# A planned instruction order and in-place operands in a fused linear-attention and MLP kernel

## The chip, the core and the metric

The program runs on one core of a Trainium2 chip. The metric is the device time of one execution in microseconds (us), as the median of several runs. TensorE (PE) multiplies, VectorE (DVE) and ScalarE (ACT) do the elementwise work, GpSimd (POOL) a little of it, and SyncE (SP) only issues the transfers between HBM and the on-chip memory (SBUF).

## The reference

A block takes x (2048 tokens by 512), normalises each token, and adds to x the result of a 32-head linear attention and of a squared-ReLU MLP, both of the normalised tokens:

```python
xn = _layernorm(x, axis=-1)
return x + _A_ref(xn, A_wqkv, A_wo) + _B_ref(xn, B_w1, B_b1, B_w2, B_b2)
# A: q, k, v = xn @ wqkv;  phi(t) = where(t > 0, t + 1, exp(t)) + 1e-6
#    kv = phi(k)^T v per head;  z = sum over tokens of phi(k)
#    o = phi(q) kv / (phi(q) z + 1e-6);  result o @ wo
# B: h = xn @ w1 + b1;  relu(h)^2 @ w2 + b2     (1376 hidden units)
```

## The kernel before

**Arithmetic.** Everything is float32. Each matmul operand is split into a high part (an ACT copy to float32r) and a rest (a DVE subtraction); `split`, L108 and L116, does it everywhere. A product is then three passes of float32r matmuls of 128x128 by 128x512. The first projections of a pair of token blocks use Strassen's scheme with seven products instead of eight; for them the weights appear as seven operands per block of 256 columns (sums and differences of quarters, then split), called "1", k, i. The second projections use operands "2", k, i: four per block for the first pair of token blocks, more combinations for the second.

**Stages.** The 16 token tiles of 128 are normalised, turned and projected to k, and the sums `kx` over all tokens are made (L439). Then comes a loop over two pairs of token blocks, `n` = 0 and 1, 512 tokens to a block. In each pair, `p` runs over seven weight blocks: two of the q projection and five of w1. An iteration does seven products (L503), copies banks of PSUM out in steps (ACT L108, DVE L990, L998, L1026), applies phi or relu and square (L540, L543, L548, L549), splits the result (`s`), and multiplies it by the second operands (L521, `add_product`). For q the denominators are made by `shares` (L558 to L566). After the loop over p come the attention products, the remaining second products and the output: transposed on DVE (L870), added to the residual `res` (L872), and stored (L877).

**Operands.** All of the weights' operands are made once, by "pieces" (`prepare_1`, `prepare_2`, `prepare_z`, and `prepare_t` in the second pair): a load of raw rows into one of four slots (`raws`, L181, L198), sums on DVE (L242, L280, L281), the split into one of four staging slots (`st`), and a store to HBM (`spill`, L203, tensors `wd`, `wdz`). Both pairs then fetch each operand back from HBM (`fetch_ops`, L453) into a ring of eight one-operand slots, 256 KB each. So what the first pair uses makes the way to HBM and back too.

**Order.** Each engine runs its instructions strictly in the order in which the program lists them. That order is written out by hand: the loop calls `hook` at fixed places, and a table `PLAN` says for each place how many steps are taken from the queues "p" (pieces), "l" (denominators), "c" (combinations for the second pair) and "s" (token sums). In the token stage a table `PIECES` does the same. SP issues all transfers, in one queue. The PSUM has eight banks in two groups of four.

Of the kernel before, what the change touches and what calls it, by code (L numbers as in the profile page):

```python
# [14 lines left out]
H = 32  # L15


@with_exitstack
def kernel(
# [29 lines left out]
    nc = tc.nc  # L49
# [17 lines left out]
    nc.scalar.preload_act_table_set("natural_log_exp_and_others")  # L67

    keep = ctx.enter_context(tc.tile_pool(name="keep", bufs=1))
    work = ctx.enter_context(tc.tile_pool(name="work", bufs=1))  # L70
    small = ctx.enter_context(tc.tile_pool(name="small", bufs=4))
    psum = ctx.enter_context(tc.tile_pool(name="psum", bufs=4, space=bass.MemoryType.PSUM))
    ctx.enter_context(tc.manual_schedule())

    def bank(name, tag="ps"):
        return psum.tile([P, 512], F32, name=name, tag=tag)
# [4 lines left out]
    turns = {"x": [0, 2], "pair": [0, 5], "raw": [0, 4], "st": [0, 4]}  # L81
# [6 lines left out]
    def two(name):  # L88
        return keep.tile([P, 2, 512], F32, name=name, tag=next_tag("x"))
# [46 lines left out]
    xT = {b: keep.tile([P, NJ, BT], F32, name=f"xT{b}", tag=f"xT{b}") for b in range(NB // 2, NB)}  # L136
    first_xp = {i0: four(f"xp{i0}", tag, pool=keep) for i0, tag in zip(range(0, NT, TB), ("B0", "B1", "C0", "C1"))}
    for k in range(2):
        two(f"x_{k}")
    for k in range(5):  # L140
        pair(f"pair_{k}")
# [28 lines left out]
    raws = {}  # L170

    def turn_of(of):
        k, n = turns[of]
        turns[of][0] = (k + 1) % n
        return k

    def raw(name, src=None):
        k = turn_of("raw")
        t = raws[k // 2][:, k % 2]
        if src is not None:  # L180
            nc.sync.dma_start(t, src)  # L181
        return t

    stages = {}

    def stage():
        k = turn_of("st")
        return stages[k // 2][:, k % 2]
# [3 lines left out]

    def columns_of(w, f, n=P):
        t = raw("r")
        tj = t.rearrange("p (j n) -> p j n", j=NJ)
        if n < P:
            nc.gpsimd.memset(tj[:, :, n:], 0.0)
        nc.sync.dma_start(tj[:, :, :n], w[:, f * P:f * P + n].rearrange("(j p) n -> p j n", j=NJ))  # L198
        return t
# [6 lines left out]
    def ops_of(kind, k, i, src, el="dve"):  # L206

        n = src.shape[1]
        t = stage()[:, :n]
# [6 lines left out]
    def prepare_z(t, i, el="dve"):  # L216
        o = v = stage()
        if len(t.shape) == 4:
            v = o.rearrange("p u (h c m) -> p u h c m", h=2, c=2)
        split(v[:, 0], v[:, 1], t, "act", el)  # L220
        spill("z", 0, i, o)

    def prepare_z1():
        t = columns_of(w1, NF - 1, FL)
        return [lambda: prepare_z(t, 0)]

    def prepare_z2():
        t = raw("r")
        nc.gpsimd.memset(t[FL:, :], 0.0)
        nc.sync.dma_start(t[:FL, :], w2[(NF - 1) * P:, :])  # L230
        nc.sync.dma_start(t[FL:FL + 1, :], b2[None, :])
        return [lambda: prepare_z(by_chunks(by_halves(t)), 2)]

    def prepare_1(k, el="dve"):

        w, f = (wqkv, 2 * k) if k < NQ else (w1, 2 * (k - NQ))
        ra, rb = (columns_of(w, f + e).rearrange("p (h n) -> p h n", h=2) for e in range(2))
        a11, a12, a21, a22 = ra[:, 0], ra[:, 1], rb[:, 0], rb[:, 1]
        held_sums = {}

        def tt(o, x, y, op):
            nc.vector.tensor_tensor(out=o, in0=x, in1=y, op=op)  # L242

        def sums_12():
            o = held_sums[0] = sums_tile(f"sa{k}")
            tt(o[:, 0], a21, a22, OP.add)
            tt(o[:, 1], o[:, 0], a11, OP.subtract)
            ops_of("1", k, 2, o, el)

        def sums_34():  # L250
            o = sums_tile(f"sb{k}")
            tt(o[:, 0], a11, a21, OP.subtract)
            tt(o[:, 1], a12, held_sums[0][:, 1], OP.subtract)
            ops_of("1", k, 4, o, el)

        return [lambda: ops_of("1", k, 0, ra, el), sums_12, sums_34, lambda: ops_of("1", k, 6, rb[:, 1:], el)]
# [9 lines left out]
    def rows_of(k):  # L266
        at = [2 * k + e for e in range(2)] if k < NP else [2 * (k - NP) + e for e in range(2)]
        return [by_halves(raw("r", w2[f * P:(f + 1) * P, :] if k < NP else wdm[f])) for f in at]

    def prepare_2(k):  # L270
        t = rows_of(k)
        return [lambda e=e: ops_of("2", k, 2 * e, by_chunks(t[e])) for e in range(2)]

    def prepare_t(k):
        b1_, b2_ = rows_of(k)
        held_sums = {}

        def step(e, x, y, z, less):
            o = held_sums[e] = sums_tile(f"t{k}_{e}")
            nc.vector.tensor_tensor(out=o[:, 0], in0=x, in1=y, op=OP.subtract)  # L280
            nc.vector.tensor_tensor(out=o[:, 1], in0=z, in1=held_sums[0][:, less], op=OP.subtract)  # L281
            ops_of("2", k, 4 + 2 * e, by_chunks(o))

        return [lambda: step(0, b1_[:, 1], b1_[:, 0], b2_[:, 1], 0), lambda: step(1, b2_[:, 1], b1_[:, 1], b2_[:, 0], 1)]

    def piece_o(j):
        t = raw(f"ro{j}", wo[j * P:(j + 1) * P, :])
# [3 lines left out]
        return [lambda: split(*wos[j + 1], t, "act", "dve")]  # L291
# [151 lines left out]
    order, loaded, ready, op_slots, op_turn = [], [], set(), [], [0, 0]  # L443
# [4 lines left out]
    def fetch_ops():  # L448

        while order and op_turn[1] < len(op_slots) and order[0] in ready:  # L450
            key = order.pop(0)
            t = op_slots[op_turn[0] % 8]
            nc.sync.dma_start(f32(t), place_of(*key))  # L453
            loaded.append((key, t))
            op_turn[0] += 1
            op_turn[1] += 1

    def order_of(n):

        o = []  # L460
        for p in range(NK + 1):
            f = p - 1 - NQ
            if p < NK:
                o += [("1", p, i) for i in range(3)]
            if f >= 0:
                o += [("2", f, i) for i in ((0,) if n else (0, 1))]
            if p:
                o.append(("1", p - 1, 6))
            if p < NK:
                o += [("1", p, 3), ("1", p, 5)]  # L470
                if n and p == 0:
                    o += [("z", 0, u) for u in range(2)]
                if f >= 0:
                    o += [("2", f, i) for i in ((2,) if n else (2, 3))]
                o.append(("1", p, 4))
        attention = [("2", NP + j // 2, 2 * (j % 2) + v) for j in range(NJ) for v in range(2)]
        z = [("z", 0, 2 + u) for u in range(2)]

        def over(i):
            return [("2", f, i) for f in range(NP)]  # L480

        if n == 0:
            o += attention + [("2", NP - 1, i) for i in (2, 3)] + z
            return o + attention + [("2", f, i) for f in range(NP) for i in range(4)] + z
        o += over(4)[:-1] + [("2", NP - 1, 2), ("2", NP - 1, 4)]
        return o + attention + z + over(5) + over(3) + over(6) + attention + z + over(7)

    def op(*key):
        assert loaded, ("late", key)
        k, t = loaded.pop(0)  # L490
        assert k == key, (k, key)
        return t

    def used(n=1):
        op_turn[1] -= n
        fetch_ops()
# [19 lines left out]
    def second(ps, key, s, first=False, last=False):  # L516

        a = op(*key)
        for n, (u, v) in enumerate(ORDER):
            for c in range(2):  # L520
                nc.tensor.matmul(ps[c], lhsT=a[:, u * 256 + c * P:u * 256 + (c + 1) * P], rhs=s[:, v],  # L521
                                 start=first and n == 0, stop=last and n == 2, skip_group_check=True)
        used()

    def second_z(ps, cs, s, first=False, last=False):
# [6 lines left out]
        used(2)  # L532
# [197 lines left out]
    order.extend([("z", 0, u) for u in range(2)] + order_of(0) + order_of(1))  # L730
# [14 lines left out]
    def fetch():  # L745
        while todo and len(held) < 3:
            held.extend(todo.pop(0)())

    def pieces(n):
        for _ in range(n):  # L750
            if held:
                held.pop(0)()
            fetch()
# [450 lines left out]
```

## Time and profile before

| what | value |
|---|---|
| median of three runs | 514.56 us (513.11 to 516.28) |
| profiled execution, its own time | 518.54 us |
| its span, first to last instruction | 516.4 us |
| outside the span | 2.1 us |
| PE busy | 443.2 us, 86% of the span |
| DVE busy | 331.0 us, 64% |
| ACT busy | 255.6 us, 49% |
| moved by DMA | 117.45 MB, mean 227 GB/s |
| mean granted TensorE clock | 0.943 |

The profile gives for each engine its busy time, and for groups of instructions their number, mean duration and the idle time in front of them with what ended it ("<-"). `PEld` is the loading of weights, which overlaps PE. `x` counts instructions. A busy PE isn't necessarily at its peak, because matmuls overlap; the number of matmuls per stretch of time says more than the busy share.

### The profile page before, as it was taken

What the parts mean: (1) busy time and instruction counts of PE and PEld (TensorE: products, weight loads), DVE (VectorE), ACT (ScalarE), POOL (GpSimd) and SP (SyncE); (2) the same over time, 40 slices, a digit from 0 to 9 for tenths busy, and PEclk for the clock granted to TensorE, in tenths of its full rate; (3) what the DMA queues carried; (4) which work ended last, traced back from release to release, by engine and by line L of the source; (5) the groups of instructions that cost most, each with busy time, mean ns of one, the idle gap of its engine ahead of it and who ended that gap; (6) DMA issues with size and microseconds to landing.
All of it is one profiled execution on the core that took longest, in us unless ns stands there. A gap on an engine that the chain in (4) does not pass through costs nothing.

```text
span 516.4 us, 5845 instructions
## 1 busy us (share of the span) xinstructions
PE 443.2 (86%) x1808; PEld 346.0 (67%) x1808; DVE 331.0 (64%) x551; ACT 255.6 (49%) x438; POOL 28.1 (5%) x48
## 2 busy tenths in 40 slices
PE   8999799999778688897989998978867855899993
PEld 7787587877557566675858887855645633687781
DVE  6999869876555668675279405545855757336843
ACT  5765556564565644755156502554564466234310
POOL 2241223200000000000000000000000000000000
PEclk9999899999888897999879999989989898799998
DMA  7834556556899899999976877776447749956853
GB/s 251 272 104 124 187 170 193 163 181 203 280 382 348 327 384 392 330 387 285 210 216 187 237 225 193 215 248 217 150 137 268 218 152 231 197 182 191 216 164 81
DMA packets 96898, 117.45 MB, mean 227 GB/s; under 512 B 42242, under 2 KB 53506, under 8 KB 96612
## 3 DMA queue, kind: packets, MB, share of 16 engines
q1 hardware_dynamic: 96868, 117.09, 73.0%
q8 instruction: 14, 0.23, 0.2%
q14 instruction: 16, 0.13, 0.1%
HBM read 81.14 MB, written 33.82 MB: 223 GB/s over the span
## 4 chain that ended last, share of the span: by engine, by line
DVE 31%; PE 28%; ACT 16%; DMA 12%; issue 7%; SPq 4%; DVEq 0%; ACTq 0%
PE acc L521 13%; DMA raws<-in_B_w_dram 5%; DVE st L116 4%; DMA ops<-wd 4%; PE b L503 4%; PE Y L521 4%; ACT st L108 4%; ACT rr L540 2%; ACT s L108 2%; DVE s L116 2%; SPq L345 2%; PE V L521 2%; DVE o L870 2%; DVE st L301 1%; ACT rr L543 1%
## 5 line engine op out<-in xcount | busy, mean ns | idle before, releaser
L521 PE MATMUL acc<-s,ops 128*128 128x512 f32 x480 | 124.4, 414 | 6.5 <-ACT s L108 3.6
L521 PEld LDWEIGHTS acc<-s,ops 128*128 128x128 f32 x480 | 95.4, 201 | 32.9 <-ACT s L108 6.7
L503 PE MATMUL b<-T,ops 128*128 128x512 f32 x336 | 91.4, 414 | 19.4 <-DVE rr L990 14.3
L503 PEld LDWEIGHTS b<-T,ops 128*128 128x128 f32 x336 | 65.0, 198 | 40.9 <-DVE rr L990 17.6
L439 PE MATMUL kx<-pk,tok 128*128 128x512 f32 x192 | 48.1, 398 | 0.4 <-DVE pk L428 0.2
L116 DVE TENSOR_TENSOR s<-rr,s 128x512 fp32r<-128x512 f32 x46 | 29.7, 686 | 24.8 <-ACT s L108 24.8
L503 PE MATMUL b<-xs1h,ops 128*128 128x512 f32 x56 | 22.9, 450 | 24.4 <-ACT rr L108 14.9
L439 PEld LDWEIGHTS kx<-pk,tok 128*128 128x128 f32 x192 | 35.6, 190 | 9.6 <-DVE pk L428 1.2
L108 ACT ACTIVATE s<-rr 128x512 fp32r<-128x512 f32 x46 | 27.4, 628 | 28.6 <-PE acc L521 15.8
L503 PE MATMUL b<-xs0h,ops 128*128 128x512 f32 x112 | 37.0, 392 | 0.1
L503 PEld LDWEIGHTS b<-xs1h,ops 128*128 128x128 f32 x56 | 11.2, 200 | 31.2 <-ACT rr L108 18.0
L116 DVE TENSOR_TENSOR st<-raws,st 128x512 fp32r<-128x512 f32 (+1 forms) x30 | 21.9, 736 | 12.8 <-ACT st L108 10.9
L521 PE MATMUL Y<-s,ops 128*128 128x512 f32 x84 | 22.8, 422 | 6.7 <-ACT s L108 4.4
L116 POOL TENSOR_TENSOR tok<-xp,tok 128x512 fp32r<-128x512 f32 x16 | 23.4, 1467 | 60.6 <-ACT tok L108 56.5
L521 PEld LDWEIGHTS Y<-s,ops 128*128 128x128 f32 x84 | 16.8, 204 | 11.8 <-ACT s L108 5.2
L503 PEld LDWEIGHTS b<-xs0h,ops 128*128 128x128 f32 x112 | 21.2, 189 | 4.9 <-DVE rr L415 0.5
L108 ACT ACTIVATE rr<-b 128x512 f32<-128x512 f32 x27 | 15.6, 582 | 14.6 <-PE b L503 14.5
L540 ACT ACTIVATE rr<-rr,b1s 128x512 f32<-128x512 f32 x15 | 10.9, 724 | 23.7 <-DVE rr L990 10.4
L503 PE MATMUL b<-xs0l,ops 128*128 128x512 f32 x56 | 21.8, 389 | 0.0
L108 ACT ACTIVATE st<-raws 128x512 fp32r<-128x512 f32 (+1 forms) x30 | 17.4, 588 | 5.4 <-DMA raws<-in_B_w_dram 5.4
L540 ACT ACTIVATE rf<-rf,b1s 128x512 f32<-128x512 f32 x10 | 7.2, 723 | 23.2 <-DVE rf L990 15.7
L549 DVE SCALAR_TENSOR_TENSOR rr<-rr,e 128x512 f32<-128x512 f32 x12 | 8.3, 692 | 14.0 <-ACT e L548 14.0
(168 smaller groups left out, 741.9 us busy)
## 6 DMA issues: line engine op xcount, KB each, us to landing
ops<-wd SPq DMA_DIRECT2D x205, 256.0 KB, 4.4
wd<-st SPq DMA_DIRECT2D x45, 512.0 KB, 5.3
raws<-in_B_w_dram SPq DMA_DIRECT2D x30, 256.0 KB, 4.6
res<-in_A_x_dram SPq DMA_DIRECT2D x32, 128.0 KB, 6.1
out_dram<-res SPq DMA_DIRECT2D x32, 128.0 KB, 3.0
ops<-wdz SPq DMA_DIRECT2D x12, 256.0 KB, 3.6
x<-in_A_x_dram SPq DMA_DIRECT2D x5, 512.0 KB, 6.4
xTd<-t SPq DMA_DIRECT2D x8, 256.0 KB, 3.6
```

The source lines that it names most:

```text
L108: nc.scalar.activation(o, i, AF.Copy, bias=bias)
L116: ENG[el].tensor_tensor(out=l, in0=src, in1=f32(h), op=OP.subtract)
L301: nc.vector.bn_stats(st[:, k, :], xr[tiles[k]])
L345: nc.sync.dma_start(*moves.pop(0))
L439: nc.tensor.matmul(kxp[c], lhsT=tok[i][:, u, c * P:(c + 1) * P], rhs=pk[i][:, v], start=i == 0 and (u, v) == first, stop=i == NT - 1 and ( ...
L503: nc.tensor.matmul(ps, lhsT=a[:, u * 256 + j * P:u * 256 + (j + 1) * P], rhs=b[v][:, j, :], start=first and j == 0 and n == 0, stop=last a ...
L521: nc.tensor.matmul(ps[c], lhsT=a[:, u * 256 + c * P:u * 256 + (c + 1) * P], rhs=s[:, v], start=first and n == 0, stop=last and n == 2, ski ...
L540: nc.scalar.activation(o, i, AF.Relu, bias=b1s[:, f:f + 1])
L543: nc.scalar.activation(r, r, AF.Square)
L549: nc.vector.scalar_tensor_tensor(p, p, 1.0, e, op0=OP.max, op1=OP.min)
L870: nc.vector.transpose(o, src)
```

## The change

**Recording.** `nc` becomes a `Program`. Its engines are recorders: a call makes a `Task` with the regions that it reads and writes, its predecessors, and a duration from a table of costs (0.0135 us + n/2400 for a matmul of n columns, 0.157 us + n/960 for a DVE `tensor_tensor`, 0.2 or 0.22 us + n/1250 for ACT, 0.06 us for the issue of a transfer, then bytes at 380 kB/us one after the other, and 1.9 us to its landing). Tiles become `Place` and `View`, and are allocated when the first instruction that uses them is given out.

**Ordering.** `order` gives each task a due time: TensorE's tasks keep the order of the program and are due one after the other; every other task is due early enough for the tasks that follow from it. Then it plays the program through: an engine that comes free takes, of its ready tasks, the one due first. Everything up to the first `kx` (`fixed`) keeps its order too. The tasks are given out by their planned start.

```python
+            else:
+                t = min((t for t in waiting[e] if t.ready <= when + 0.1), key=lambda t: (t.due, t.index))
+                waiting[e].remove(t)
+            t.start = max(when, t.ready)
...
+        return sorted(ts, key=lambda t: (t.start, t.index))
```

`hook`, `PLAN`, `PIECES` and the queues go; their steps are recorded at once where they arise.

**Operands of the first pair.** The ring becomes eight slots of two operands (`D0` to `D7`, 512 KB each). `needed_in(n)` lists the entries in their order of use. In the first pair an entry is made in its slot (`make_1`, `make_2`, `make_z`), used from there, and stored to HBM for the later uses; it isn't fetched. The operands `make_t` of the second pair pass through the ring too, on their way to HBM. The other entries are fetched, two operands with one transfer where they are neighbours.

```python
+        def both_of(kind, k, i, make=None):
+            o.append(([(kind, k, i), (kind, k, i + 1)], make))
...
+            direct = n == 0
             if p < NK:
-                o += [("1", p, i) for i in range(3)]
...
+                both_of("1", p, 0, make_1(p, 0) if direct else None)
+                both_of("1", p, 2, make_1(p, 2) if direct else None)
```

The staging slots `st` are gone. Raw weights are loaded 512 KB at a time into two tiles (`rp0`, `rp1`), and two more (`x0`, `x1`) once the attention's values are done; a tile is reloaded when its last operand is made (`raw_done`).

**Smaller edits.** The loads of the residual are recorded elsewhere and land in other tiles, with another layout (`r[g, h]`). In the very last second product (`end`) the three passes of the first output bank come before those of the second:

```python
-        for n, (u, v) in enumerate(ORDER):
-            for c in range(2):
...
+        for n, (u, v), c in [(n, uv, c) for c in range(2) for n, uv in enumerate(ORDER)] if end else \
+                [(n, uv, c) for n, uv in enumerate(ORDER) for c in range(2)]:
```

The compiled programs compare as follows. Both have 1722 matmuls of 128x512 and 59 smaller ones, 551 DVE and 437 ACT instructions of the same kinds and sizes. The transfers fall from 444 to 304: 217 fetches of one operand (256 KB) become 47 of two and 42 of one, and 30 loads of w1, w2 with 256 KB each become 10 with 256 KB (column blocks) and 10 with 512 KB (row blocks); the 54 stores of operands remain.

More of the change, by code (lines that the diff above doesn't have):

```diff
@@ L15, with __init__, real @@
 H = 32
+REORDER = True
+class Task:
+    __slots__ = ("engine", "name", "args", "kw", "preds", "succs", "dur", "lag", "lock", "due", "ready", "left", "start", "at",
+                 "index", "size")
+class Place:
+    def __init__(self, pool, tag, shape, dt, name, last):
+        self.pool, self.tag, self.shape, self.dt, self.name, self.last = pool, tag, shape, dt, name, last
+        self.tasks, self.tile = [], None
+    def real(self):
+        if self.tile is None:
+            self.tile = self.pool.tile(self.shape, self.dt, name=self.name, tag=self.tag)
+        return self.tile
@@ L30 @@
 ):
-    nc = tc.nc
+    nc = Program(tc.nc)
+    nc.apart = out.tensor.name
     xf = x.rearrange("b s d -> (b s) d")
@@ L135 @@
     xsb = [both(f"xs{n}", (f"xs{n}h", f"xs{n}l")) for n in range(2)]
[L136 to L141, printed above, removed]
+    xT = {b: work.tile([P, NJ, BT], F32, name=f"xT{b}", tag=f"xT{b}") for b in range(NB // 2, NB)}
+    first_xp = {i0: four(f"xp{i0}", tag, pool=work if tag[0] == "r" else keep) for i0, tag in zip(range(0, NT, TB), ("B0", "B1", "r4", "r5"))}
     dram = ctx.enter_context(tc.tile_pool(name="dram", bufs=1, space=bass.MemoryType.DRAM))
@@ L264, in by_chunks, with make_z, make @@
         return t.rearrange("p h (m c) -> p h c m", c=2)
[L266 to L284, printed above, removed]
+    def make_z(i):
+        def make(o):
+            t, v = raw_of[f"z_{i}"][0][:, 0], o
+            if i:
+                v, t = o.rearrange("p u (h c m) -> p u h c m", h=2, c=2), by_chunks(by_halves(t))
+            split(v[:, 0], v[:, 1], t, "act", "dve")
+            spill("z", 0, 2 * i, o)
+            raw_done(f"z_{i}")
+        return make
@@ new lines, with tt, make_1, make @@
+    held_sums = {}
+    def tt(o, x, y, op=OP.subtract):
+        nc.vector.tensor_tensor(out=o, in0=x, in1=y, op=op)
+    def make_1(k, i):
+        def make(o):
+            t = raw_of[f"1_{k}"][0]
+            ra, rb = (by_halves(t[:, e]) for e in range(2))
+            a11, a12, a21, a22 = ra[:, 0], ra[:, 1], rb[:, 0], rb[:, 1]
+            if i == 0:
+                src = ra
+            elif i == 6:
+                src = rb[:, 1:]
+            else:
+                src = held_sums["1", k, i] = sums_tile(f"s{i}_{k}")
+                if i == 2:
+                    tt(src[:, 0], a21, a22, OP.add)
+                    tt(src[:, 1], src[:, 0], a11)
+                else:
+                    tt(src[:, 0], a11, a21)
+                    tt(src[:, 1], a12, held_sums["1", k, 2][:, 1])
+            ops_of(o, "1", k, i, src)
+            left[f"1_{k}"] = left.get(f"1_{k}", 4) - 1
+            if not left[f"1_{k}"]:
+                raw_done(f"1_{k}")
+        return make
@@ new lines, with make_2, make, make_t @@
+    left = {}
+    def make_2(k, e):
+        def make(o):
+            ops_of(o, "2", k, 2 * e, by_chunks(by_halves(raw_of[f"2_{k}"][0][:, e])))
+            if e:
+                raw_done(f"2_{k}")
+        return make
+    def make_t(k, e):
+        def make(o):
+            (b11, b12), (b21, b22) = ((t[:, 0], t[:, 1]) for t in (by_halves(raw_of[f"t_{k}"][0][:, e]) for e in range(2)))
+            src = held_sums["t", k, e] = sums_tile(f"t{k}_{e}")
+            if e == 0:
+                tt(src[:, 0], b12, b11)
+                tt(src[:, 1], b22, src[:, 0])
+            else:
+                tt(src[:, 0], b22, b12)
+                tt(src[:, 1], b21, held_sums["t", k, 0][:, 1])
+            ops_of(o, "2", k, 4 + 2 * e, by_chunks(src))
+            if e:
+                raw_done(f"t_{k}")
+        return make
@@ L458, in order_of, with load_keys, make, advance @@
-    def order_of(n):
+    def load_keys(keys):
+        def make(t):
+            (kind, k, i), two_of = keys[0], len(keys) == 2
+            if two_of and keys[1] == (kind, k, i + 1):
+                nc.sync.dma_start(f32(t), place_of(kind, k, slice(i, i + 2)))
+            else:
+                for e, key in enumerate(keys):
+                    nc.sync.dma_start(f32(t[:, e]), place_of(*key))
+        return make
+    def advance():
+        while needed and free_ops:
+            keys, make = needed[0]
+            if make is None and not ready.issuperset(keys):
+                break
+            needed.pop(0)
+            tag = free_ops.pop(0)
+            t = keep.tile([P, 2, 512], F32R, name="ops", tag=tag)
+            (make or load_keys(keys))(t)
+            holder = [len(keys), tag]
+            for e, key in enumerate(keys):
+                loaded.setdefault(key, []).append((t[:, e], holder))
+            if not keys:
+                free_ops.append(tag)
@@ L926 @@
         if n:
-            raws.update({k: two(f"raws{k}") for k in range(2)})
-            todo = [lambda k=k: prepare_t(k) for k in range(NP)]
+            raw_free[:] = ["x0", "x1"]
+            raw_jobs += [raw_2(k, "t") for k in range(NP)]
+            fetch_raws()
         banks = [bank(f"b{n}_{k}", loop_tag) for k in range(4)]
@@ L1140, in strassen @@
         def strassen(ps, k, i, first=False, last=False):
[L1141 removed]
+            return lambda: h[k][i], lambda s: second(ps, ("2", k - NQ, i), s, first, last, i == 7 and last)
         def phase_jobs(ps, i, first=False, last=False):
```

554 lines of the change are left out of this document (366 added, 188 removed).

## The prediction

> **What bounds the kernel now.** I read the page first, then busy time by stage, then PE's waits in the two loops. Busy tenths, granted clock (PEclk) and DMA share in 40 slices:
>
> ```profile
> PE   8999799999778688897989998978867855899993
> PEclk9999899999888897999879999989989898799998
> DMA  7834556556899899999976877776447749956853
> ```
>
> No one engine bounds all of it. I cut the span where the first q product starts (110.8), where the first pair's last loop product ends (242.2), at the second pair's first product (309.8), at its loop's end (432.9) and near the last product (508). Columns: start:end, length, then busy us and (xinstructions) of PE, PEld, DVE, ACT, POOL, the clock, DMA share, GB/s.
>
> ```profile
> 0.00:110.80 110.80, 106.19 (x462) 85.37 (x463) 92.51 (x172) 67.59 (x131) 27.61 (x47) 0.98 0.58 177
> 110.80:242.20 131.40, 110.69 (x447) 85.66 (x445) 84.32 (x139) 73.24 (x122) 0.52 (x1) 0.92 0.95 335
> 242.20:309.80 67.60, 62.42 (x254) 50.39 (x254) 33.10 (x42) 26.83 (x41) 0.00 (x0) 0.92 0.79 210
> 309.80:432.90 123.10, 97.28 (x373) 71.90 (x371) 76.59 (x130) 62.27 (x100) 0.00 (x0) 0.94 0.66 204
> 432.90:508.00 75.10, 66.42 (x277) 52.65 (x276) 41.80 (x67) 25.65 (x44) 0.00 (x0) 0.95 0.71 185
> 508.00:516.40 8.40, 0.17 (x1) 0.00 (x0) 2.71 (x4) 0.00 (x0) 0.00 (x0) 0.76 0.28 64
> 8.04 1.02 PE L420 MATMUL pk<-wkh,xs1h 128*128 128x512 f32 x2 [0.17 <-ACT xs1h L378]
> 119.93 3.73 PE L840 MATMUL pkv<-kxs,wv 128*128 128x128 f32 x32
> 487.97 1.36 PE W L521 x6
> ```
>
> The last row, from the chain that ended last, gives PE's pace when nothing stops it: six matmuls in 1.36 us, 0.227 each. By the program's count the first loop has 414 wide matmuls and 32 small ones (97.4 us: 414 x 0.227, and 3.5 of the 3.73 for the small, whose end overlaps what follows), its remaining jobs 252 (57.1), the second loop 372 (84.3), its remaining jobs 276 (62.6). The stages take 131.4, 67.6, 123.1 and 75.1. So the loops lose 34 and 39 us, the jobs 10 and 12; the token stage loses about 8 (432 matmuls and transposes, 94.6 us, in the 102.8 from its first projection, the row at 8.04, to 110.8).
>
> The loops lose for different reasons. In the first, DMA is busy 95% of the time at 335 GB/s; in the second 66%. PE's waits in the two:
>
> ```profile
> PE b L503 <- ACT rf L108: 9.7, 4, 4.2
> PE b L503 <- DVE rr L990: 5.8, 2, 3.5
> PE b L503 <- DMA ops<-wd: 2.7, 3, 1.2
> PE b L503 <- ACT rr L108: 15.9, 10, 3.9
> PE b L503 <- DVE rr L990: 8.5, 6, 2.6
> ```
>
> The first three are the first loop's, the others the second's (us, times, longest). PE itself hardly waits for DMA, but the instruction that releases it stands behind others that do. How, a stretch of the second loop shows:
>
> ```profile
> 379.91 0.42 DVE L281 TENSOR_TENSOR t<-raws,t 128x256 f32<-128x256 f32 x1
> 380.36 0.66 ACT L108 ACTIVATE st<-t 128x512 fp32r<-128x512 f32 x1 [1.43 <-DVE t L281]
> 380.93 0.58 ACT L108 ACTIVATE rr<-b 128x512 f32<-128x512 f32 x1
> 381.56 0.50 PE L503 MATMUL b<-xs1h,ops 128*128 128x512 f32 x1 [3.74 <-ACT rr L108]
> ```
>
> ACT stood 1.43 us waiting for a sum of a weight that is wanted much later, and only then copied out the bank that PE had waited 3.74 us for. The blocks therefore come 20 us apart, in both loops:
>
> ```profile
> 168.50 0.70 DVE c L998
> 187.99 0.70 DVE c L998
> 376.16 0.70 DVE rr L998
> 396.39 0.70 DVE rr L998
> ```
>
> Such a block has 66 matmuls in the first loop (15.0 us) and 54 in the second (12.2).
>
> **The change part by part: traffic.** No instruction of PE, ACT or DVE goes or comes; 217 fetches of 256 KB (0.262 MB) become 47 double and 42 single ones.
>
> ```profile
> ops<-wd SPq DMA_DIRECT2D x205, 256.0 KB, 4.4
> wd<-st SPq DMA_DIRECT2D x45, 512.0 KB, 5.3
> raws<-in_B_w_dram SPq DMA_DIRECT2D x30, 256.0 KB, 4.6
> res<-in_A_x_dram SPq DMA_DIRECT2D x32, 128.0 KB, 6.1
> ```
>
> That is 136 x 0.262 = 35.6 MB in place of 56.9, 21 MB less. Some 67 of the fetches that go lie in the first loop: 17.6 of its 44.0 MB (335 GB/s x 131.4). The 26.4 left need 75 us at the 353 GB/s of a full DMA (335/0.95): below PE's 97. A block moved 26 times 0.262 MB: 4 of raw weights in, 11 operands out, the same 11 back in. These 6.8 MB take 19 us at that rate, which is what set its 20 us; without the 11 it is 3.9 MB, 11 us. The first loop's bound passes to PE.
>
> **Order.** What then sets a loop is how well in-order engines keep PE fed. A stretch and a steady stage of this profile show how well that can go:
>
> ```profile
> 202.00:222.00 20.00, 18.59 (x81) 14.50 (x80) 14.94 (x25) 12.06 (x20) 0.52 (x1) 1.00 0.98 344
> ```
>
> Here 81 matmuls ran in 20 us, 92% of the pace, with DVE 75% busy. I take these as two bounds: PE at 92% for the near side, DVE at 75% for the far side.
> First loop: 97.4/0.92 = 106 us, or 84.3/0.75 = 112. I take 110, near the far end, since its first two blocks have the token sums and the values to make and no second products to hide them: 21 saved.
> Second loop: 84.3/0.92 = 92, or 76.6/0.75 = 102. Its three bank copies and adds per block have at least six matmuls (1.36 us) of cover each, and what is to be put first costs little:
>
> ```profile
> L108 ACT ACTIVATE rr<-b 128x512 f32<-128x512 f32 x27 | 15.6, 582 | 14.6 <-PE b L503 14.5
> L540 ACT ACTIVATE rr<-rr,b1s 128x512 f32<-128x512 f32 x15 | 10.9, 724 | 23.7 <-DVE rr L990 10.4 <-DVE rr L1026 9.3 <-DVE rr L998 3.9
> L543 ACT ACTIVATE rr<-rr 128x512 f32<-128x512 f32 x20 | 12.6, 632 | 0.6
> L108 ACT ACTIVATE s<-rr 128x512 fp32r<-128x512 f32 x46 | 27.4, 628 | 28.6 <-PE acc L521 15.8 <-PE W L521 8.3 <-PE W L530 2.1
> ```
>
> A copy is 0.58 us; the longest chain, bias, square and head of `s` for `add_product(p - 1, 1)`, is 0.72 + 0.63 + 0.63 = 2.0 us against 2.7 us of PE work (twelve matmuls) that lies between. So no chain forces a wait; ACT (62.3 of 84.3) and DVE (76.6 of 84.3) are only nearly full. Its traffic is unchanged, 3.9 MB a block, 11 us at 353 GB/s. I take 99: 24 saved.
>
> **Jobs, tokens, end.** The remaining jobs lose at their starts:
>
> ```profile
> 258.07 5.95 DMA ops<-wdz
> 436.62 1.52 PE L521 MATMUL Y<-s,ops 128*128 128x512 f32 x4 [3.59 <-ACT s L108]
> 440.45 4.94 PE L521 MATMUL Y<-s,ops 128*128 128x512 f32 x13 [2.30 <-DVE s L116]
> 507.98 0.72 DVE L870 STREAM_TRANSPOSE o<-V 128x512 f32<-128x512 f32 x1 [2.17 <-PE V L521]
> ```
>
> The first pair's `z` operand is made in place now, so its fetch (5.95 us of the chain) goes; the second pair's first `s` splits no longer stand behind combinations (L967). At 92%: 57.1/0.92 = 62 and 62.6/0.92 = 68, so 6 and 7 saved (bounds: 0, if these waits only move, and 10 and 12). In the token stage DVE is 92.5 of 110.8 us busy, so little is to be had: 3, between -4 (the residual's loads now stand in SP's queue ahead of block 1's weights) and 8. The reordered last product frees its first bank three matmuls earlier: 0.7. DVE's planned sharing of time with POOL, recording and allocation cost no instruction: 0.
>
> **Sum.** 3 + 21 + 6 + 24 + 7 + 0.7 = 61.7. Against the profiled execution's own 518.5 us (516.4 and 2.1 around it) that gives 456.8. The runs' median is 0.8% lower than that execution (514.56), so 453; I say 454.
>
> **The rivals.**
> *The waits change place in the second loop.* Traffic is relieved in the first loop, but the second, with DVE at 76.6 and ACT at 62.3 us, stays at 123 and its jobs at 75: 24 + 7 less, 485. For it: no traffic goes there, and ring entries of `make_t` take two of seven per block. Against: its long waits are for a 0.58 us copy behind work that isn't due.
> *Near PE's pace.* All stages at 97% of it (104, 100, 59, 87, 65, end 7.7) give a span of 423 and 422 us by the runs. For it: the clock is 0.91 to 0.92 in the gappy stages and 1.00 in that dense stretch, so closed gaps give back more than themselves. Against: three other engines would have to be over 85% busy without once being late. The Trainium skill (TensorE: Matmul & The Clock Gate, "What's actually happening") says the clock halves only after an idle window of about 3.4 us; by that rule waits below it would leave the full clock, and this end would need only the 3.5 to 4.2 us waits to go. The trace gives the clock as a mean over stretches, which fits this but doesn't show it.
> *Late landings, slower.* The planner issues a transfer in 0.06 us and lands 512 KB in 1.9 + 0.524/0.38 = 3.3 us. The trace has 5.3 (`wd<-st`) and this for issues:
>
> ```profile
> 174.49 2.71 SPq L453 DMA_DIRECT2D ops<-wd  x5
> 428.93 6.62 SPq L865 DMA_DIRECT2D res<-in_A_x_dram  x8
> ```
>
> 0.54 us an issue, 0.48 more than planned: with eight a block 3.8 us, and 2.0 for the landing, 5.8 us late per block. If a making copy on ACT stands there waiting for its raw weights, the bank copies listed behind it wait as well, and 14 blocks lose 81 us: 535. It turns slower than before at 4.3 us a block (60/14). Against: four raw tiles let a load go out about a block (15 us) ahead of its use. That engines can't step past a waiting instruction is what the trace showed at 380 us; the Trainium skill (TensorE: Matmul & The Clock Gate, specifications at its head) has ACT and DVE as strict FIFOs too, eight deep, which speaks for this rival and against a plan by assumed times.
> *It does nothing*, because the hand-written table was as good and DMA not the bound: within 1% (about what a measurement of this kernel can tell from no change).
>
> **How the numbers follow.** Forecast 0.57 (438 to 472), waits change place 0.21 (475 to 500), near PE's pace 0.09, slower 0.10, nothing 0.03. Faster by over 1% is the sum of the first three, 0.87. The range 430 to 496 leaves out the slower and idle cases (0.13) and a few hundredths at each end, 0.2 in all.
>
> **What would show it.** Right: DMA share in the first loop near 0.7, 27 MB instead of 44; blocks 16 us apart there and 14 in the second; no PE wait over 2 us for ACT L108's bank copy; clock near 1.00 in both loops; the second loop near 99 us with DVE over 75% busy. Wrong: DVE or ACT idle for seconds of a block "<-DMA raw" with PE waiting behind it, or `L453`-like fetches landing after PE asks for them in the second loop; then the plan's transfer times are the step that failed.

## The result, and the profile after

The changed kernel takes 447.09 us (445.99 to 448.68) beside 513.84 us (512.86 to 516.28) of the kernel before on the same chip: 0.870 of the time, 95% interval 0.866 to 0.874. The forecast was 454. The profiled execution took 448.7 us, its span 446.7. All medians below are of all runs of a kernel; the ratios leave out two runs, one of the kernel "list order, fetched back" and one of the kernel that is only aligned, which fell in a slower state of the core.

From the page of after: busy times, and in 40 slices PE, the granted clock and the DMA share. Every recorded instruction now has the line of the recorder, L249, so groups are told apart by tiles.

```profile
PE 419.8 (94%) x1808; PEld 336.9 (75%) x1808; DVE 323.9 (73%) x551; ACT 255.4 (57%) x438; POOL 28.8 (6%) x48
...
PE   8999497699999999999999999999899999999992
...
PEclk9999889889999999999999999999999999999997
DMA  7853404950487977677592998698777899858705
```

From the ninth slice on PE has no slice under 8 up to the last, and from the tenth on the clock has none under 9. The holes that are left, in slices five, seven and eight, lie in the token stage.

The stages of both kernels, cut at the starts of the same matmuls (first q product, first matmul of the first pair's jobs, of the second pair's loop, of its jobs, and the end; the jobs so begin 2.6 and 3.7 us later than in the prediction's cut, since a wait ahead of them counts to the loop). Columns as in the prediction; before, then after:

```profile
0.00:110.81 110.81, 106.20 (x462) 85.37 (x463) 92.52 (x172) 67.59 (x131) 27.61 (x47) 0.98 0.58 177
110.81:244.83 134.02, 110.69 (x448) 85.67 (x446) 84.86 (x140) 75.76 (x127) 0.52 (x1) 0.92 0.95 331
244.83:309.80 64.97, 62.41 (x253) 50.38 (x254) 32.56 (x42) 24.31 (x37) 0.00 (x0) 0.92 0.79 214
309.80:436.62 126.82, 97.42 (x373) 71.90 (x372) 78.07 (x133) 65.76 (x107) 0.00 (x0) 0.95 0.66 202
436.62:508.17 71.55, 66.46 (x276) 52.65 (x276) 40.49 (x65) 22.16 (x38) 0.00 (x0) 0.95 0.69 186
```

```profile
0.00:124.06 124.06, 109.25 (x462) 87.32 (x463) 90.84 (x169) 69.04 (x132) 28.25 (x47) 0.94 0.51 146
124.06:223.59 99.53, 99.53 (x447) 81.33 (x446) 86.14 (x149) 82.86 (x139) 0.52 (x1) 1.00 0.76 265
223.59:283.17 59.58, 58.86 (x254) 47.26 (x253) 28.27 (x40) 16.16 (x24) 0.00 (x0) 1.00 0.82 264
283.17:373.43 90.26, 87.45 (x373) 69.27 (x371) 77.50 (x133) 63.97 (x106) 0.00 (x0) 1.00 0.87 267
373.43:438.89 65.46, 64.74 (x276) 51.69 (x276) 39.08 (x60) 23.33 (x39) 0.00 (x0) 1.00 0.65 170
```

The loops give 34.5 and 36.6 us, the jobs 5.4 and 6.1, the end 0.4 (8.2 to 7.8). The token stage takes 13.3 back. In the first loop PE is never idle, and the DMA moves 26.4 MB (265 GB/s x 99.53) where before it moved 44.4.

Where the token stage loses, by the waits of PE and DVE (total, times, longest) and a stretch of the timeline:

```profile
PE acc L249 <- ACT pk L249: 6.3, 2, 4.1
PE ps L249 <- DVE xs0l L249: 6.2, 1, 6.2
PE acc L249 <- DMA ops<-wd: 0.2, 1, 0.2
DVE xT L249 <- DMA xg<-xp: 15.3, 2, 9.2
```

```profile
40.20 12.14 SPq L249 DMA_DIRECT2D xg<-xp  x16
53.85 0.71 DVE L249 STREAM_TRANSPOSE xT<-xg 128x512 f32<-128x512 f32 x1 [9.22 <-DMA xg<-xp]
54.72 0.69 DVE L249 TENSOR_TENSOR xs0l<-ps,xs0h 128x512 fp32r<-128x512 f32 x1
55.46 2.08 PE L249 MATMUL ps<-wkh,xs0l 128*128 128x512 f32 x4 [6.16 <-DVE xs0l L249]
```

SP needs 12.14 us to issue sixteen moves of 64 KB, 0.76 each; the plan gave 0.06 each, about 1 us together. So DVE's transposes of `xg` were listed some 11 us too early (an estimate from these two numbers), and DVE, which can't step past, stood 9.22 us with `xs0l`, which was ready to be made, behind them. The same again at 77 us (6.09 us, PE 4.14). In the kernel before the same sixteen moves took nearly as long, but DVE waited for them 1.8 us in all (the timeline, and the group of transposes by line):

```profile
39.63 10.81 SPq L345 DMA_DIRECT2D xg<-xp  x16
```

```profile
L349 DVE STREAM_TRANSPOSE xT<-xg 128x512 f32<-128x512 f32 x8 | 5.6, 703 | 2.0 <-DMA xg<-xp 1.8 <-issue 0.2
```

### The profile page after: what moved, and what is told of

It is laid out like the page before. It is cut to its first block, busy times and chain, and to the rows that moved or that the text cites. A ratio compares the mean times of both kernels' runs of the same rounds, so it can differ in the third digit from the quotient of the medians.

```text
span 446.7 us, 5498 instructions
## 1 busy us (share of the span) xinstructions
PE 419.8 (94%) x1808; PEld 336.9 (75%) x1808; DVE 323.9 (73%) x551; ACT 255.4 (57%) x438; POOL 28.8 (6%) x48
## 4 chain that ended last, share of the span: by engine, by line
PE 77%; DMA 7%; DVE 4%; SPq 4%; ACT 4%; issue 1%; DVEq 0%
PE ps L249 43%; PE acc L249 34%; SPq L249 4%; DMA wd<-ops 2%; DMA xTd<-t 1%; ACT rr L249 1%; DMA raw<-in_A_wqkv_dram 1%; DMA ops<-wd 1%; ACT s L249 1%; DVE xp L249 1%; ACT k L249 1%; DMA x<-in_A_x_dram 1%; ACT ops L249 0%; DVE ops L249 0%; DMA xg<-xp 0%
## 5 line engine op out<-in xcount | busy, mean ns | idle before, releaser
L249 PE MATMUL ps<-s,ops 128*128 128x512 f32 x390 | 95.3, 395 | 0.7 <-ACT s L249 0.7
L249 PEld LDWEIGHTS ps<-s,ops 128*128 128x128 f32 x390 | 73.1, 188 | 18.9 <-ACT s L249 1.6
L249 PE MATMUL acc<-s,ops 128*128 128x512 f32 x300 | 74.5, 396 | 2.2 <-ACT s L249 1.4
L249 PEld LDWEIGHTS acc<-s,ops 128*128 128x128 f32 x300 | 56.1, 188 | 16.6 <-ACT s L249 2.3
L249 PE MATMUL acc<-pk,tok 128*128 128x512 f32 x192 | 51.8, 421 | 6.5 <-ACT pk L249 6.3
L249 PEld LDWEIGHTS acc<-pk,tok 128*128 128x128 f32 x192 | 37.8, 202 | 17.0 <-issue 7.1
L249 ACT ACTIVATE s<-rr 128x512 fp32r<-128x512 f32 x46 | 28.5, 628 | 25.6 <-PE acc L249 13.9
L249 PE MATMUL ps<-T,ops 128*128 128x512 f32 x168 | 42.4, 395 | 0.0
L249 DVE TENSOR_TENSOR s<-rr,s 128x512 fp32r<-128x512 f32 x46 | 31.2, 685 | 15.4 <-ACT s L249 14.3
L249 PE MATMUL acc<-T,ops 128*128 128x512 f32 x168 | 42.2, 395 | 0.0
L249 PEld LDWEIGHTS acc<-T,ops 128*128 128x128 f32 x168 | 31.5, 188 | 7.6 <-ACT rr L249 0.2
L249 PEld LDWEIGHTS ps<-T,ops 128*128 128x128 f32 x168 | 31.5, 188 | 7.4
L249 POOL TENSOR_TENSOR tok<-xp,tok 128x512 fp32r<-128x512 f32 x16 | 23.8, 1490 | 48.4 <-ACT tok L249 38.5
L249 ACT ACTIVATE rr<-acc 128x512 f32<-128x512 f32 x23 | 13.5, 588 | 19.4 <-PE acc L249 19.1
L249 PE MATMUL ps<-xs0h,ops 128*128 128x512 f32 x72 | 23.8, 391 | 0.0
L249 ACT ACTIVATE ops<-raw 128x512 fp32r<-128x512 f32 (+1 forms) x28 | 16.3, 590 | 8.1 <-DMA raw<-in_A_wqkv_dram 4.5
L249 PE MATMUL acc<-xs0h,ops 128*128 128x512 f32 x56 | 18.7, 394 | 1.3 <-DVE t L249 1.2
L249 DVE TENSOR_TENSOR ops<-raw,ops 128x512 fp32r<-128x512 f32 (+1 forms) x28 | 19.1, 696 | 1.1 <-ACT ops L249 1.1
L249 DVE SCALAR_TENSOR_TENSOR k<-ps,k 128x512 f32<-128x512 f32 x16 | 10.9, 682 | 9.6 <-ACT k L249 9.6
L249 DVE STREAM_TRANSPOSE xT<-xg 128x512 f32<-128x512 f32 x8 | 5.6, 704 | 15.3 <-DMA xg<-xp 15.3
L249 DVE TENSOR_TENSOR rr<-acc,rr 128x512 f32<-128x512 f32 x21 | 14.3, 681 | 3.0 <-PE acc L249 2.0
L249 ACT ACTIVATE k<-ps 128x512 f32<-128x512 f32 x16 | 9.5, 591 | 12.2 <-PE ps L249 12.1
```

Source lines behind the costliest of these rows:

```text
L249: getattr(getattr(self.nc, t.engine), t.name)(*map(real, t.args), **{k: real(a) for k, a in t.kw.items()})
```

## The experiments

Four questions: what each half of the change is worth alone; whether the planner's issue cost is what the token stage lost; whether its landing costs too; and why PE, never idle in the first loop, still needs 0.232 us a matmul there.

Stage lengths by the same marks (token, loop, jobs, loop, jobs, end), and the median of each kernel (the kernel before had 513.8 to 515.5 in the groups of runs):

| kernel | token | loop 1 | jobs 1 | loop 2 | jobs 2 | end | median us |
|---|---|---|---|---|---|---|---|
| before | 110.8 | 134.0 | 65.0 | 126.8 | 71.5 | 8.2 | 513.8 |
| after | 124.1 | 99.5 | 59.6 | 90.3 | 65.5 | 7.8 | 447.1 |
| in place, order of the program | 123.3 | 143.2 | 59.9 | 166.2 | 70.7 | 7.5 | 574.0 |
| list order, fetched back | 120.4 | 179.8 | 82.0 | 92.1 | 65.5 | 7.8 | 548.2 |
| the same, six slots to fetch into | 119.9 | 177.8 | 84.0 | 95.0 | 65.5 | 7.8 | 548.6 |
| the same with measured costs | 111.4 | 184.3 | 84.3 | 96.4 | 65.4 | 7.8 | 553.8 |
| list order, fetched back, made ahead | 121.6 | 147.7 | 59.6 | 91.9 | 65.5 | 7.8 | 493.2 |
| after, measured issue | 111.7 | 99.5 | 59.6 | 92.2 | 65.5 | 7.6 | 437.5 |
| after, measured landing | 115.1 | 99.5 | 66.6 | 91.5 | 65.5 | 7.6 | 448.0 |
| measured issue, aligned | 111.0 | 98.1 | 58.4 | 90.1 | 63.9 | 7.2 | 430.7 |
| measured issue and landing, aligned | 111.8 | 97.4 | 60.2 | 95.7 | 64.0 | 6.9 | 436.2 |

**In place, without the list order.**

```diff
-REORDER = True
+REORDER = False
```

> The changed kernel with its operands used in place, but given out in the order in which the program records them: no list order. Theory A (the order does most in both loops, the traffic only lifts a ceiling): the weights' splits are recorded where a slot comes free, ahead of the bank copies that PE waits for, so the loops lose what they lost before or more: second loop 115 to 130 us, first loop 115 to 130, total 490 to 520. Rival B (the traffic was the bound and in-place operands do most): first loop stays near 100 us, total 455 to 475.

Measured: 573.96 us (572.43 to 574.39), ratio 1.115 (1.108 to 1.122): slower than before, and outside both ranges: theory A had the cause, but put the loss far too low. (The old hand-written queues are gone in this kernel too, so it shows the recorded order, not the old one with operands in place.) Its second loop, where the traffic is that of the kernel before, takes 166 us. PE's longest wait and its cause, from the timeline:

```profile
338.55 0.42 DVE L249 TENSOR_TENSOR t<-raw_t 128x256 f32<-128x256 f32 x1 [7.16 <-DMA raw_t<-in_B_w_dram]
339.51 0.66 ACT L249 ACTIVATE ops<-t 128x512 fp32r<-128x512 f32 x1 [10.98 <-DVE t L249]
343.64 0.66 ACT L249 ACTIVATE ops<-t 128x512 fp32r<-128x512 f32 x1 [3.47 <-DMA wd<-ops]
347.86 1.06 ACT L249 ACTIVATE rr<-acc 128x512 f32<-128x512 f32 x2
348.49 0.80 PE L249 MATMUL acc<-xs1h,ops 128*128 128x512 f32 x1 [16.52 <-ACT rr L249]
```

Making steps for later operands stand in front: ACT waits 10.98 us for a sum of weights that were still landing, and 3.47 for a slot to be stored. The bank copy `rr<-acc` behind them keeps PE waiting for 16.52 us. It is the pattern that the prediction showed at 380 us of the kernel before, four times as long.

**List order, first-pair operands stored and fetched back.**

```diff
+            for e, (keys, make) in enumerate(o):
+                back += [(None, make), (keys, None)] if make else [(keys, make)]
...
-    free_ops += [f"D{k}" for k in range(8)]
+    free_ops += [f"D{k}" for k in range(4)]
```

An entry is made in one of `D4` to `D7`, stored, and fetched into one of `D0` to `D3`; once the last is made, all eight are for fetches.

> List order kept; in the first pair the operands are made in four of the eight slots, stored, and fetched back from HBM into the other four, as before the change (217 fetched operands again, the memory shared as before). Theory A: the first loop must move 26 times 0.262 MB per block again and is bound by DMA at about 19 us a block: first loop 120 to 130 us in place of 99.5, all else as in the changed kernel, total 467 to 480. Rival B' (PE waited there for ACT's order alone, DMA kept up): within 5 us of the changed kernel, 445 to 452.

Measured: 548.19 us (544.17 to 554.59), ratio 1.061 (1.051 to 1.071). Neither expectation held. The second pair is nearly as fast as in the changed kernel; the first loop takes 179.8 us though the DMA is only 74% busy there (120.39 to 300.18), so bandwidth is not the reason:

```profile
120.39:300.18 179.79, 118.45 (x447) 92.06 (x446) 96.07 (x155) 87.68 (x142) 0.52 (x1) 0.82 0.74 248
```

PE waits for the fetches instead:

```profile
PE ps L249 <- DMA ops<-wd: 56.6, 9, 12.6
```

Two variants asked whether there were too few slots, or whether the plan's costs were off. The first makes in two slots and fetches into six, the second also has the measured costs of transfers (below).

> List order, first-pair operands stored and fetched back as in the fetch-back kernel (548 us), but with two slots to make them in and six to fetch into, in place of four and four. Theory H (the loop waits for the round trip, make, store, land, fetch, because too few fetches can be out at once): two more slots shorten the waits, 490 to 525 us, the first loop 130 to 155 in place of 180. Rival I (bandwidth, 11 fetches a block): 540 to 555, DMA share in the first loop over 0.9. Rival J (the makes wait for the store of the slot they take): 555 to 590 and waits of ACT or DVE for the store.

Measured: 548.57 us (544.97 to 551.99), ratio 1.065 (1.059 to 1.070). Rival I's time came, but not its cause: the DMA is 72% busy in the first loop. Rival J's sign is there, ACT waiting 48.5 us in that loop for the store of one of the two slots that it makes in, so this variant doesn't test the slots to fetch into by themselves.

> The kernel with two slots to make in and six to fetch into, with the planner's transfers at measured cost (issue 0.7 and 0.5 us, landing 3.5 us plus the bytes). Theory H (slots): within 10 us of the six-and-two kernel. Theory K (the order is planned with fetches that land too soon, so that work waiting for them stands ahead of work that is ready): 455 to 490, PE's waits for ops<-wd under 20 us.

Measured: 553.79 us (551.42 to 555.47), ratio 1.074 (1.071 to 1.078). Neither the other split of the slots nor the planned costs cure it. What was left stood in the waits of SP's own queue, in the first kernel of these three between 120 and 300 us:

```profile
SPq L249 <- DVE made L249: 38.7, 13, 8.9
SPq L249 <- DMA wd<-made: 38.7, 13, 5.9
```

For 77 us SP stood at the fetch of an operand whose making or store wasn't finished, and every other transfer behind it. So I moved each making and store four made entries ahead of its fetch:

```diff
+            made = [(None, make) for keys, make in o if make] + [(None, None)]
+            back += made[:4]
+            del made[:4]
             for e, (keys, make) in enumerate(o):
-                back += [(None, make), (keys, None)] if make else [(keys, make)]
+                if make and made:
+                    back.append(made.pop(0))
+                back.append((keys, None))
```

> The fetch-back kernel (four slots to make in, four to fetch into, list order) with every operand made and stored four made entries ahead of its fetch, instead of directly before it. Theory L (in the fetch-back kernel SP's in-order queue stood 77 us between 120 and 300 us for the making and for the landing of the store of the very entry that it was to fetch next, with every other fetch behind): these waits fall under 30 us, the first loop from 180 to 120-150 us, the time from 548 to 485-520. Rival M (bandwidth, or too few slots for a landing of 4.7 us): SP's waits move to its free slots, first loop over 170, 535 to 555.

Measured: 493.22 us (492.30 to 495.97), ratio 0.954 (0.946 to 0.963): the theory of the waiting queue holds, with the same four and four slots. From 115 to 275 us SP waits 20.2 us for `DVE made` and 0.2 for `DMA wd<-made`. Its waits for slots that PE still reads are 56.3 us there (42.0 in the first kernel of the three, 120 to 300 us). The first pair's jobs are back at 59.6 us. In the first loop the DMA is 89% busy, with 46.5 MB (315 GB/s x 147.66) where the changed kernel moved 26.4, and PE waits 32.4 us in the whole run for fetched operands:

```profile
121.55:269.21 147.66, 112.89 (x447) 86.79 (x446) 97.70 (x159) 86.92 (x142) 0.52 (x1) 0.90 0.89 315
```

```profile
PE ps L249 <- DMA ops<-wd: 20.0, 7, 9.6
PE acc L249 <- DMA ops<-wd: 12.4, 8, 2.8
```

So the list order alone, with traffic as before, is worth 22 us (515.51 to 493.22 on the same chip): 35 in the second loop and 11 in the jobs, less 11 in the token stage and 14 in the first loop; why the first loop is slower than in the old order was not tested. Operands used in place are worth some 46 more, all in the first loop. Most of that is traffic, by an estimate: 46.5 MB take 131 us at the 354 GB/s of a full DMA (315/0.89), 32 us more than the 99.5 of the changed kernel's loop. What the fewer slots to fetch into add to it, no run separates. Neither half alone gives the whole gain: the list order without a lead of the stores, and the operands in place without the list order, are both slower than before.

**The planner's issue cost.** The time for SP's issue of a transfer in the plan set to what the trace shows:

```diff
-t.size, t.dur, t.lag = 4 * b, 0.06, 1.9
+t.size, t.dur, t.lag = 4 * b, 0.7 if 4 * b <= 131072 else 0.5, 1.9
```

> The changed kernel with one number of the planner changed: a transfer's issue occupies SP for 0.7 us (128 KB or less) or 0.5 us, as the trace has it, in place of 0.06. Theory C (the token stage lost 13 us because the plan puts DVE's turns of xg long before sixteen moves can be issued, and PE's operands stand behind them): PE's two waits of 6.2 and 4.1 us go, the token stage falls from 124 to 112 to 116 us, total 434 to 440. Rival D (the token stage is lost to the shared work of splits and residual loads in front of it, not to the plan's transfer times): token stage 121 to 126, total 445 to 450.

Measured: 437.54 us (436.27 to 439.65), ratio 0.851 (0.845 to 0.856), as theory C has it. The moves are no faster, but the long waits behind them are gone; DVE waits 1.7 us for `xg` in place of 15.3. The issue of the moves, and PE's longest waits for ACT:

```profile
39.75 12.35 SPq L249 DMA_DIRECT2D xg<-xp  x16
```

```profile
PE ps L249 <- ACT xs1h L249: 2.2, 1, 2.2
PE acc L249 <- ACT pk L249: 1.5, 1, 1.5
```

The Trainium skill (DMA: Bandwidth & Descriptors, "Issuing engines are not separate DMA queues") says the time a sequencer takes to start a transfer is usually small beside the transfer. For these moves it isn't small in the trace: 0.77 us of issue each, beside about 2.0 us to the landing of 64 KB, and 12.35 us for sixteen one after the other.

**The planner's landing.** Instead, only the landing made longer (`t.lag` 1.9 to 3.5).

> The changed kernel with the planner's landing of a transfer at 3.5 us after its bytes in place of 1.9, issues still at 0.06. Theory C says issue time, not landing, is what the token stage lacks: 16 moves are 12 us of issue and 2 us of landing, so the waits shrink by at most 1.6 us each: total 441 to 448. Rival E (late landings everywhere cost as much): the loops' last waits go too, total 432 to 440.

Measured: 448.00 us (446.59 to 448.94), ratio 0.870 (0.865 to 0.876), the same as the changed kernel. Theory C's total came, but not its reason: the token stage gains 8.9 us, where waits shorter by at most 1.6 us each were expected. So what that stage lacked is planned time until the moves have landed; put into the issue it gives 12.4 us, put into the landing 8.9. The total stays because the first pair's jobs lose 7.0 us. PE's two longest waits, the first in the token stage, the second in these jobs:

```profile
PE acc L249 <- DVE pk L249: 5.7, 2, 5.3
PE ps L249 <- DMA ops<-wd: 5.0, 1, 5.0
```

Of the fetches that the changed kernel issues around the start of the jobs (four from 222.38 to 231.00 us, the jobs starting at 223.59), this plan issues two; the next go out 22 us into the jobs, behind eight loads of the residual. The granted clock is 0.50 in the 3.4 us behind the wait.

**The pace of a matmul.** In the changed kernel matmuls that wait for nothing start 0.232 us apart, before 0.227. From the addresses in the compiled programs: before, the moving operand and the weights of 1710 of the 1722 wide matmuls begin at the same byte offset modulo 64; after, those of 1080 differ by 32 bytes, since tiles are placed as they are first used and small ones lie between. One pool more holds the small tiles apart, and moves no instruction:

```diff
+    tiny = ctx.enter_context(tc.tile_pool(name="tiny", bufs=1))
...
-            place = last_place[tag] = Place(self.pool, tag, shape, dt, name, last_place.get(tag))
+            place = last_place[tag] = Place(tiny if n % 16 else self.pool, tag, shape, dt, name, last_place.get(tag))
```

> The changed kernel with the small tiles in a pool of their own and nothing else. Theory F (offsets): 439 to 442 us in place of 447, pace 227 ns. Rival G (list order): 445 to 449, pace 232 to 234.

Measured: 439.63 us (437.27 to 443.96), ratio 0.852 (0.850 to 0.855). The order of instructions on every engine is the same as in the changed kernel, and all 1722 wide matmuls have equal offsets.

> The changed kernel with the planner's measured issue times (0.7 us for a move of up to 128 KB, 0.5 us for a larger one) and, besides, all tiles smaller than 64 bytes per partition, and those of odd multiples of 32 bytes, in a pool of their own, so that the moving operand and the weights of every wide matmul begin at the same byte offset modulo 64. No instruction goes or comes. Theory F (the pace of a wide matmul depends on that: 227 ns where the offsets agree, 234 where they differ): pace 227 ns in all stages and about 1080 x 6 ns = 6 us less than the kernel with measured issue times alone (437.5): 429 to 433. Rival G (the 234 ns come from the list order's mixing of streams, not from addresses): pace stays at 232 to 234 and the time at 436 to 439.

Measured: 430.72 us (428.45 to 432.76), ratio 0.836 (0.833 to 0.839). A stretch of the first loop on the chain that ended last, in the changed kernel, and then in this one:

```profile
172.26 5.55 PE ps L249 x24
177.81 2.75 PE acc L249 x12
...
187.54 5.55 PE ps L249 x24
```

```profile
158.95 5.44 PE ps L249 x24
164.39 2.72 PE acc L249 x12
...
173.91 5.44 PE ps L249 x24
```

24 matmuls take 5.55 and 5.44 us (0.231 and 0.227 each), a block of 66 15.28 and 14.96. The changed kernel shows it by itself, too: its 642 wide matmuls with equal offsets start 228 ns before the next matmul (median), the 1080 others 235. By the medians aligning saves 7.5 us without and 6.8 with the measured issue cost, by the ratios to before 9.0 and 7.6. This is the fastest of the kernels here.

**Both measured costs, aligned.** `t.lag` at 3.5 as well:

> The kernel with measured issue times and aligned operands (430.7 us), with the planned landing also set to the measured one (3.5 us plus the bytes, in place of 1.9). If late landings still cost something in the plan: 422 to 428. If the landing is covered already, or moves the operands of the remaining jobs as it did alone (66.6 in place of 59.6 us): 430 to 438.

Measured: 436.19 us (435.54 to 438.13), ratio 0.844 (0.837 to 0.851): slower than without. Its second loop takes 95.7 us for 90.1, with PE waiting 6.2 us for fetched operands. A more faithful number for one term made the whole plan worse.

## Why the prediction was right, and where not

The direction and the size were right (447 for 454, in the likeliest case's own 438 to 472), but the sum holds two errors that offset each other: the loops gave 71 us by the marks used here, 65 by the prediction's own, where 45 were counted; and the token stage took 13 where 3 were to be gained. That the total came within 7 us is in part luck.

*Traffic, first loop: right.* 26.4 MB forecast, 26.4 measured; the bound passed from DMA to PE as said. The fetched-back kernel with a lead shows the other side: with traffic back, its first loop keeps the DMA 89% busy and takes 48 us more, some 32 of them by the estimate above for bytes alone.

*Order, the two loops: the mechanism was right, the term mis-sized.* The step that failed is the pair of bounds, "PE at 92%" and "DVE at 75% busy". In the changed kernel's first loop:

```profile
140.00:160.00 20.00, 20.00 (x88) 16.19 (x87) 17.50 (x34) 17.29 (x32) 0.00 (x0) 1.00 0.83 296
160.00:180.00 20.00, 20.00 (x88) 16.21 (x87) 18.49 (x35) 16.83 (x29) 0.00 (x0) 1.00 0.82 283
```

DVE is 88 to 92% busy, ACT 84 to 86%, and PE has no gap. What the best stretch of the old kernel showed (81 matmuls in 20 us, DVE 75%) was what its order reached, not what the engines can do. So from the first loop on it went as in the case "near PE's pace": that said 100, 59, 87 and 65 us for these stages (99.5, 59.6, 90.3 and 65.5 came), and 104 for the token stage, which took 124.1. Against it stood that three more engines would have to be over 85% busy without once being late; DVE was, ACT nearly, and the stores and loads kept up.

*The token stage: outside its bounds* (3 saved, from -4 to 8; 13.3 lost). The prediction had the mechanism, an issue planned at 0.06 us and measured at 0.54, and used it in a rival of late landings in the loops only. It put into the token stage's bound just the residual's loads. The row with the sixteen `xg<-xp` issues in 10.81 us stood in the trace of the kernel before, and the prediction doesn't use it; the first wait of 9.22 us is for just these. Setting the issue cost takes 12.4 us off that stage (124.1 to 111.7), beside 110.8 before, so the list order itself gains nothing there. In the loops, where the rival expected 5.8 us late per block, little was late: PE waits 0.2 us in all for fetched operands, and no wait of PE there is over 1.2 us; that the four raw tiles gave the lead, as was said against it, no run tested. The mechanism itself, a making copy that stands with the bank copies behind it, is what the kernel in the order of the program shows.

*Jobs and end.* 6 and 7 counted, 5.4 and 6.1 came by the marks used here, 8.2 and 8.9 by the prediction's own; the waits at their starts went, as said. The end gave 0.4 for 0.7.

*What would show it.* Blocks in the first loop 15.3 us apart (16 said), in the second 12.6 to 13.5 (14 said); DMA share 0.76 (0.7); clock 1.00 from there to the last jobs; no wait of PE over 2 us for the bank copy; second loop 90 us (99 said) with DVE 86% busy. The clock rose with the gaps closed: 0.92 and 0.95 in the loops before, 1.00 after. By these means the low clock had cost at most 11 us of the first loop (0.08 x 134.0) and 6 of the second (0.05 x 126.8), an estimate, of the 34.5 and 36.6 that they gave; so most of the gain is the waits themselves. The stages behind the token stage, in which PE never waits longer than 1.2 us, have the full clock. Shorter waits than the 3.5 to 4.2 us that the prediction names are enough to lose it. In the changed kernel's token stage PE waits 2.19 us, and soon after the clock is 0.50 for 3.41 us:

```profile
86.89:89.08 2.19, 0.00 (x1) 0.03 (x1) 1.43 (x3) 2.19 (x5) 0.00 (x0) 1.00 0.47 193
90.57:93.98 3.41, 3.41 (x10) 2.64 (x9) 3.32 (x7) 1.88 (x5) 0.26 (x1) 0.50 0.44 120
```

Matmuls there start 0.43 us apart (93.07, 93.50, 93.93). The kernel before shows the same after a wait of 2.63 us (clock 0.50 from 58.42 to 61.83). The rule of the Trainium skill that was weighed there (TensorE: Matmul & The Clock Gate, "What's actually happening") has the clock fall only after an idle window of some 3.4 us. For these two waits the traces differ from it, so the prediction's reading, by which waits below 3.4 us leave the full clock, does not hold in this kernel.

*Still open.* The 5 ns per matmul lost to addresses weren't in the sum at all (about 7 us). Why the second loop loses 5.6 us with a longer planned landing was not followed up, beyond one wait of 5.8 us for a fetched operand. Operands used in place in the old hand-written order were not run either: the kernel in the order of the program has lost that order, so what they are worth without the list order stays open.

## What to carry to other kernels

A planned order is as good as the planned times of the thing that waits longest: check its constants (issue per transfer, landing) against rows of a trace, in every stage that issues many small transfers, and judge each new number by the whole time, since one truer term can make the plan worse. Undoing half of a change needs the lead that the old code had, or the experiment measures its own new wait: the fetched-back kernel gave 548 us until its stores ran four entries ahead, and 493 then. And a best stretch of an old trace bounds what its order reached, not what the engines can do.

## What the hardware showed that was not expected

A wide matmul in float32r takes 227 ns when its moving operand and its weights begin at the same byte offset modulo 64 (both at 0, or both at 32, as in the kernel with the program's order), and 234 to 235 ns when one begins at 0 and the other at 32; with all 1722 at the same offset the loops run at 0.227 again. The Trainium skill (TensorE: Matmul & The Clock Gate, "Wait — 56ns, not 53.3ns?") gives 215.7 ns for 512 columns with the full clock; both paces here are slower, at a granted clock of 1.00. SP needs 0.76 us to issue each of sixteen 64 KB moves `xg<-xp` in a row (0.63 in the second sixteen, 10.08 us together) and 0.56 each for eight 128 KB loads, but 0.32 for one move of 1 MB, `xT<-xTd`; the time doesn't go by the bytes:

```profile
76.01 4.50 SPq L249 DMA_DIRECT2D res<-in_A_x_dram  x8
118.43 0.32 SPq L249 DMA_DIRECT2D xT<-xTd  x1
```
